# Unread matmuls in the loading phase, earlier loads of two batches, and one place for the second softmax's products

## The chip, the cores and the metric

One core of a Trainium2 chip runs the kernel. The metric is the device time of one execution in microseconds, lower is better. A second, profiled execution gives the trace that the times of single instructions come from.

## The reference

Batch 8, 8 heads, 512 tokens and 32 state rows per head, head size 64; the feed-forward part has 1536 hidden columns. Two softmax attentions are computed between tokens and state, and their results, 544 rows a batch, go through a gated feed-forward layer:

```python
scores = scale * x @ state.T          # 512 x 32 per head
a = softmax(scores); xread = a @ state
scores2 = scale * state @ x.T         # 32 x 512 per head
a2 = softmax(scores2); sread = a2 @ x
y = concat([xread, sread], rows)      # per batch 544 rows of 8 * 64 columns
out = (sigmoid(y @ w_gate) * (y @ w_val)) @ w_out
```

## The kernel before

All tensors are cast to bf16 for TensorE. `xread` is never formed: since `xread @ w = a @ (state @ w)`, the kernel multiplies the small state by the weights once a batch (`sw_wide`, `sw_visit`, result `SW`) and then the transposed probabilities `aT` by `SW` (`gv_mm`, line L283). The sigmoid is a tanh on ScalarE (`gv_th`), the gate product runs on VectorE (`gv_glu`), and `out_mm` (L314) multiplies by `w_out`.

Every instruction's place on its engine is written out by hand (`manual_schedule`): each engine works strictly in the order of the program text, and waits there for what it needs. Tiles come from pools with few buffers; a tile waits for the readers of the buffer that it takes over. In PSUM, `p_gv` has two buffers, `p_sw` four, `p_out` and `p_at` one each. `stg`, which holds x as it is loaded, has three, `Eb` two, `res` four.

**The loading phase** (up to `for b in range(2, B + 1)`) is a list of single calls. Batches 1 and 0 come first: their x is loaded in pieces by SyncE's queue (SP), cast, transposed on TensorE (`xT_mm`, L105), and goes through the scores and the first softmax, while the weights and the state arrive on GpSimd's queue (POOL). `warm(n, place)` (L348) issues n matmuls of 128 x 128 x 128 on a constant tile, into a PSUM tile that nobody reads.

**The steps.** The last loop runs over b = 2 to 8 and, inside, over the twelve column groups f of 128 hidden columns. In step b, group f issues `gv_mm(b, f)`, its tanh and gate product, and one third of an output tile of batch b - 1 (`out_mm(b - 1, f)`). Around this the step prepares the next batch, nb = b + 1:

- groups 0 and 6: `sw_wide(nb, ...)`, state times weights; its copies are spread over the following groups.
- groups 0 to 5 (1 to 6 while b < 4): `row(nb, t)`, the first softmax, ending in `aT_dma(nb)`, four transposing DMAs on SP from `ab` to `aT`.
- groups 7 to 11: `col(nb, t)`, the second softmax, ending in `c_dma(nb)`, two transposing DMAs on SP from `cN` to `Eb`.
- `load_x(b + 3)` on SP in group 8 (b = 2) or 6 (b = 3 and 4); `cast_x(b + 2)` on POOL and `at_xT_dma(b + 2)`, four transposing DMAs on SP, in group 1 (6 for b = 2).
- `sr_mm(b)`, 16 matmuls of 64 columns, the second softmax's product with x, into a PSUM tile `srp`; `sr_cp(b, 0, act)` and `sr_cp(b, 1, vec)` copy it to `XS` on ScalarE and VectorE. For b of 2 and 3 they stand in groups 9 and 10 and use `p_sw`; for b of 4 to 7 in groups 3 and 4, with `p_at`.

Step 7 has no next batch; it runs the second softmax of batches 0 and 1 instead (`col(0, f)`, `col(1, f - 3)`, with `sr_mm(0)` in group 8 and `sr_mm(1)` in group 11). Step 8 does the feed-forward of all `sread` rows, `XS`, in one go (L286).

Of the kernel before, what the change touches and what calls it, by code (L numbers as in the profile page):

```python
# [16 lines left out]
def kernel(  # L17
# [15 lines left out]
    B, H, S, D = x.shape  # L33
# [30 lines left out]
    AT, OU, GV, SWP = (p_at, "at"), (p_out, "outp"), (p_gv, "gv"), (p_sw, "swp")  # L64
# [5 lines left out]
    def load_x(b, eng, parts=1):  # L70
        xf = xfs[b] = stg.tile((128, H, 4, D), FP, name="xf")
        v, n = x[b].rearrange("h (p c) d -> p h c d", c=4), H // parts
        for i in range(parts):
            eng.dma_start(xf[:, n * i:n * i + n], v[:, n * i:n * i + n])

    def load_w(w, lo, n):
        src = (moe_w_gate, moe_w_val)[w].rearrange("(k p) n -> p k n", p=128)
        nc.gpsimd.dma_start((wg, wv)[w][:, :, lo:lo + n], src[:, :, lo:lo + n])
# [9 lines left out]
    def cast_x(b, cp, lo, n):  # L88
        if b not in xbs:
            xbs[b] = xp.tile((128, 4, H, D), BF, name="xb" if b > 1 else "xb01", bufs=3 if b > 1 else 2)  # L90
        cp(xbs[b].rearrange("p c h d -> p h c d")[:, lo:lo + n], xfs[b][:, lo:lo + n])  # L91


    def xT_tile(b):
        if b not in xTs:
            xTs[b] = ap_.tile((128, 4, 4, 128), BF, name="xT" if b > 1 else "xT01")
        return xTs[b]
# [9 lines left out]
    def xT_cp(b, j, cp):  # L107
        cp(xT_tile(b)[:, j], held["xT", b, j])
# [6 lines left out]
    def S_mm(b, i, place, jjs=(0, 1)):  # L115
        if jjs[0] == 0:
            held["S", b, i] = place[0].tile((128, 4, 2, 2, Ns), FP, name="Sp", tag=place[1])
        ps = held["S", b, i]
        for jj in jjs:
            for c in range(4):  # L120
                nc.tensor.matmul(ps[:, c, :, jj], xTs[b][:, 2 * i + jj, c], sTz[:, b, 2 * i + jj], start=True, stop=True)  # L121

    def S_max(b, i):

        if b not in E1s:
            E1s[b] = ap_.tile((128, 4, 2, 4, Ns), FP, name="E1")
        ps = held["S", b, i].rearrange("p c e j n -> p (c e) j n")
        mx = held["mx", b, i] = ap_.tile((128, 8, 2), FP, name="mx")
        nc.vector.tensor_reduce(mx, ps, AX.X, ALU.max)  # L129
# [81 lines left out]
    def sr_mm(b, place):  # L211
        sr = held["sr", b] = place[0].tile((128, 4, 2, Ns), FP, name="srp", tag=place[1])
        Eb = Ebs[b].rearrange("p c e (j n) -> p c e j n", n=Ns)
        for j in range(4):
            for c in range(4):
                nc.tensor.matmul(sr[:, j], xbs[b][:, c, 2 * j:2 * j + 2].rearrange("p h d -> p (h d)"),  # L216
                                 Eb[:, c, :, j], start=(c == 0), stop=(c == 3))
# [32 lines left out]
    def sw_wide(b, v):  # L250

        if b not in SWs:
            SWs[b] = fp.tile((128, 2, 2, dff), BF, name="SW", bufs=2)
        lo = 768 * v
        for k, places in enumerate(((OU, AT), (SWP, SWP), (SWP, SWP))):
            pss = [p[0].tile((128, 512), FP, name="swp", tag=p[1]) for p in places]
            if k < 2:
                sw_mm(pss, b, k, lo, 512, 0)
            else:
                for w in range(2):  # L260
                    sw_mm(pss, b, w, lo + 512, 256, 256 * w)
            for e in range(2):
                if k < 2:
                    sw_left[b, v, k, e] = (SWs[b][:, e, k, lo:lo + 512], pss[e])
                else:
                    sw_left[b, v, k, e] = (SWs[b][:, e, :, lo + 512:lo + 768], pss[e].rearrange("p (w n) -> p w n", w=2))

    def sw_cp(b, lo, w, e, cp):
        cp(*sw_left.pop((b, lo, w, e)))  # L269
# [5 lines left out]
    def gv_mm(b, f, place):  # L275
        n = n_of(b)
        fs = slice(f * 128, (f + 1) * 128)
        pss = []
        for w in range(2):
            ps = place[0].tile((128, 512), FP, name="gvp", tag=place[1])[:, :n]  # L280
            if b < B:
                for g in range(2):
                    nc.tensor.matmul(ps, SWs[b][:, g, w, fs], aTs[b][:, :, g], start=(g == 0), stop=(g == 1))  # L283
            else:
                for j in range(4):
                    nc.tensor.matmul(ps, (wg, wv)[w][:, j, fs], XS[:, j], start=(j == 0), stop=(j == 3))  # L286
            pss.append(ps)
        held["gv", b, f] = pss

    def gv_th(b, f):  # L290

        th = held["th", b, f] = fp.tile((128, 512), FP, name="th")[:, :n_of(b)]
        nc.scalar.activation(th, held["gv", b, f][0], AF.Tanh, scale=0.5)  # L293

    def gv_glu(b, f):
        if b not in glus:
            glus[b] = fp.tile((128, NF, n_of(b)), BF, name="glu", bufs=2, padded_shape=(128, NF, 512))
        nc.vector.scalar_tensor_tensor(glus[b][:, f], held["th", b, f], 1.0, held["gv", b, f][1], ALU.add, ALU.mult)  # L298
# [45 lines left out]
    def warm(n, place):  # L344

        ps = place[0].tile((128, 512), FP, name="warm", tag=place[1])
        for _ in range(n):
            nc.tensor.matmul(ps[:, :128], ones[:, 0], ones[:, 0], start=True, stop=True)  # L348
# [8 lines left out]
    def load_sb(q):  # L357
        sbs[q] = stg.tile((128, 1, 4, D), BF, name="sb", bufs=4)
        nc.gpsimd.dma_start(sbs[q][:, 0], state[2 * q:2 * q + 2].rearrange("b h (u l) d -> (b h u) l d", l=4))
# [5 lines left out]
    def sT_mm(q, place):  # L365
        ps = stp[q] = place[0].tile((128, 4, 64), FP, name="stp", tag=place[1])
        for l in range(4):
            for e in range(2):
                nc.tensor.matmul(ps[e * 64:(e + 1) * 64, l], sbs[q][:, 0, l], ident_e[:, e], start=True, stop=True)
# [74 lines left out]
    load_w(0, 0, 256)  # L444
    cast_x(1, vec, 4, 2)
    nc.vector.memset(sTz, 0.0)
    sT_mm(0, SWP)
    load_x(0, nc.sync, 4)
    cast_x(1, act, 2, 2)
# [10 lines left out]
    cast_x(0, vec, 0, 2)  # L460
    cast_x(0, pool, 4, 2)
    xT_cp(1, 1, act)
    S_mm(1, 0, GV)
    S_max(1, 0)
    xT_cp(1, 3, act)
    S_mm(1, 1, GV)
    S_max(1, 1)
    cast_x(0, act, 2, 2)
# [12 lines left out]
    warm(8, SWP)  # L481
    load_sb(3)
    load_w(0, 512, 512)
    S_mm(0, 0, GV, (0,))
    S_mm(0, 0, AT, (1,))
    S_exp(1, 1)
# [205 lines left out]
    for b in range(2, B + 1):  # L692
        nb = b + 1 if b + 1 < B else None
        for f in range(NF):

            v, q = divmod(f, 6)
            if nb is not None and q == 0:
                sw_wide(nb, v)
                sw_cp(nb, v, 0, 0, act)
                sw_cp(nb, v, 0, 1, act)  # L700
            ahead = nb is not None and q == 0
            for first in (ahead, not ahead):
                if first:
                    gv_mm(b, f, SWP if b == B and f % 2 else GV)
                    gv_th(b, f)
                    gv_glu(b, f)
                elif b < B or f < 9:
                    out_mm(b - 1, f)
            if nb is not None:
                if q == 0:  # L710
                    sw_cp(nb, v, 1, 0, vec)
                if q in (1, 3, 4):
                    k = max(q + 1, 3)
                    sw_cp(nb, v, k // 2, k % 2, act)
                if f == (4 if b > 3 else 10):
                    sr_cp(b, 0, act)
                    sr_cp(b, 1, vec)
                if 0 <= f - (b < 4) < 6:
                    row(nb, f - (b < 4))
                elif f >= 7:  # L720
                    col(nb, f - 7)
                if f == (6 if b > 2 else 8) and nb + 2 < B:
                    load_x(nb + 2, nc.sync, 4 if nb + 3 == B else 1)
                if f == (1 if b > 2 else 6) and nb + 1 < B:
                    cast_x(nb + 1, pool, 0, 4)
                    cast_x(nb + 1, pool, 4, 4)
                    at_xT_dma(nb + 1)
            if b < B and f == (3 if b > 3 else 9):
                sr_mm(b, AT if b > 3 else SWP)
            if b == B - 1:  # L730
                if f == 4:
                    sr_cp(b, 0, act)
                    sr_cp(b, 1, vec)
                for k in range(2):
                    if 0 <= f - 3 * k < 5:
                        col(k, f - 3 * k)
                    elif f == 8 + 3 * k:
                        sr_mm(k, SWP)
                        sr_cp(k, 0, act)
                        sr_cp(k, 1, vec)  # L740
# [33 lines left out]
```

## Time and profile before

| | |
|---|---|
| median of the timed runs | 234.08 us |
| the three timed runs | 233.50, 234.08, 234.56 us |
| profiled execution | 233.25 us |
| its span, first to last instruction | 231.5 us |
| mean granted TensorE clock in it | 0.993 |
| TensorE matmul busy (PE) | 221.3 us, 96% |
| VectorE (DVE) | 138.2 us, 60% |
| ScalarE (ACT) | 143.0 us, 62% |
| GpSimd (POOL) | 71.6 us, 31% |

A row of the timeline has the start from the span's beginning, the length, the engine, the line, the operation, its output and inputs with their shapes, and the number of equal instructions that it merges; in brackets stands how long the engine sat idle ahead of it, and what ended that. SPq and POOLq are issues to DMA queues; their length is the time of issue, not of the transfer. The end of a matmul is modelled: it overlaps the start of the next one, so short waits of PE show as a late start, or as a row that is longer than others of its form, and not as idle time.

### The profile page before, as it was taken

Reading aid. Unit: us, or ns where it says so; the run is one execution under the profiler, and the core shown is the slowest. Engines: PE = TensorE matmul, PEld = TensorE weight load, DVE = VectorE, ACT = ScalarE, POOL = GpSimd, SP = SyncE. Lnnn points to the kernel's source line nnn. Section 1 sums busy time; section 2 is a strip of 40 time slices with the busy share of each in tenths; the row PEclk is TensorE's granted clock in tenths of the full one; section 3 lists DMA queues with packets and bytes.
Section 4 is the critical chain, followed back from the end, with each engine's and each line's share of the span. In section 5 each row is a group of like instructions: output and inputs, shape, how many; then the busy total and the mean of one; then the engine's idle time right before and its main releaser. Section 6 shows DMA issues by size and latency. Waiting matters only on the chain.

```text
span 231.5 us, 4984 instructions
## 1 busy us (share of the span) xinstructions
PE 221.3 (96%) x1887; PEld 110.6 (48%) x1887; DVE 138.2 (60%) x266; ACT 143.0 (62%) x288; POOL 71.6 (31%) x77
## 2 busy tenths in 40 slices
PE   7679999999999999998999999999999999999994
PEld 7463444434544444444444454444444444566743
DVE  0889679766586558754865477648755664422311
ACT  3688787668485857584666767594847655423311
POOL 4986380320515053305330623041302246000001
PEclk9979999999999999999999999999999999999999
DMA  6999969835791459456862844213112312311113
GB/s 204 278 201 287 199 90 202 239 82 125 182 224 50 71 140 224 75 145 187 170 170 55 276 80 128 63 75 91 46 37 93 100 27 76 109 42 70 45 32 107
DMA packets 47271, 29.49 MB, mean 127 GB/s; under 512 B 29872, under 2 KB 42544, under 8 KB 47248
## 3 DMA queue, kind: packets, MB, share of 16 engines
q1 hardware_dynamic: 40096, 21.84, 37.4%
q0 software_dynamic: 6864, 7.14, 16.7%
q8 instruction: 15, 0.25, 0.5%
q10 hardware_dynamic: 288, 0.20, 0.4%
q14 instruction: 8, 0.07, 0.1%
HBM read 18.35 MB, written 8.91 MB: 118 GB/s over the span
## 4 chain that ended last, share of the span: by engine, by line
PE 79%; DVE 7%; DMA 4%; ACT 4%; POOL 2%; issue 2%; SPq 1%; ACTq 0%; DVEq 0%; POOLq 0%
PE outp L314 33%; PE gvp L283 31%; PE gvp L286 5%; PE swp L231 4%; DVE glu L298 3%; DMA Eb<-cN 2%; DMA xf<-in_x_dram 2%; PE srp L216 2%; POOL cN L204 1%; PE cTp L181 1%; ACT th L293 1%; PE outp L334 1%; PE Sp L121 1%; DVE rs L144 1%; ACT SW L269 1%
## 5 line engine op out<-in xcount | busy, mean ns | idle before, releaser
L298 DVE SCALAR_TENSOR_TENSOR glu<-th,gvp 128x512 bf16<-128x512 f32 (+1 forms) x108 | 70.3, 657 | 71.6 <-ACT th L293 52.8
L314 PE MATMUL outp<-wo,glu 128*128 128x512 bf16 x396 | 99.0, 379 | 0.0
L283 PE MATMUL gvp<-aT,SW 128*128 128x512 bf16 x384 | 97.4, 379 | 1.5 <-DMA aT<-ab 0.6
L293 ACT ACTIVATE th<-gvp 128x512 f32<-128x512 f32 (+1 forms) x108 | 61.8, 576 | 52.9 <-PE gvp L283 43.5
L283 PEld LDWEIGHTS <-SW 128*128 128x128 bf16 x384 | 36.3, 98 | 47.0 <-issue 6.2
L314 PEld LDWEIGHTS <-glu 128*128 128x128 bf16 x396 | 36.6, 98 | 40.7 <-issue 2.8
L204 POOL TENSOR_SCALAR cN<-cE,rc 128x512 bf16<-128x512 f32 x16 | 24.9, 1564 | 64.5 <-DVE rc L201 55.7
L269 ACT CAST SW<-swp 128x512 bf16<-128x512 f32 x74 | 41.1, 586 | 3.9 <-PE swp L231 2.8
L318 ACT ACTIVATE res<-outp 128x512 f32<-128x512 f32 x33 | 19.7, 597 | 17.2 <-PE outp L314 17.1
L152 POOL TENSOR_TENSOR ab<-E,ri 128x512 bf16<-128x512 f32 x16 | 16.7, 1047 | 42.5 <-DVE ri L146 34.8
L91 POOL CAST xb<-xf 128x1024 bf16<-128x1024 f32 (+1 forms) x14 | 13.6, 987 | 15.0 <-PE gvp L283 6.6
L269 DVE CAST SW<-swp 128x512 bf16<-128x512 f32 x22 | 14.8, 681 | 0.9 <-PE swp L231 0.9
L196 ACT ACTIVATE cE<-cTp,nb 128x512 f32<-128x512 f32 x16 | 11.1, 694 | 1.2 <-POOL cN L204 1.2
L144 DVE TENSOR_REDUCE rs<-E 128x16 f32<-128x512 f32 x16 | 10.8, 676 | 0.8 <-ACT E L137 0.7
L188 DVE TENSOR_REDUCE cm<-cTp 128x1 f32<-128x512 f32 x16 | 10.9, 683 | 0.4 <-PE cTp L181 0.4
L137 ACT ACTIVATE E<-E 128x512 f32<-128x512 f32 x16 | 10.1, 638 | 1.6 <-DVE E L134 1.6
L129 DVE TENSOR_REDUCE mx<-Sp 128x16 f32<-128x512 f32 x16 | 10.7, 675 | 0.4 <-PE Sp L121 0.4
L134 DVE TENSOR_TENSOR E<-Sp,mx 128x512 f32<-128x512 f32 x16 | 10.9, 685 | 0.1
L325 POOL DMA_DIRECT2D out_dram<-res x2 | 1.1, 550 | 29.7 <-ACT res L318 29.7
L231 PE MATMUL swp<-wg,sTc 64*32 64x512 bf16 (+1 forms) x192 | 8.4, 328 | 0.2
L231 PEld LDWEIGHTS <-sTc 64*32 64x32 bf16 x384 | 4.8, 91 | 7.4 <-issue 4.7
L121 PEld LDWEIGHTS <-xT 128*128 128x128 bf16 x128 | 6.0, 100 | 4.4 <-issue 1.0
(62 smaller groups left out, 134.3 us busy)
## 6 DMA issues: line engine op xcount, KB each, us to landing
out_dram<-res SPq DMA_DIRECT2D x31, 256.0 KB, 2.4
xf<-in_x_dram SPq DMA_DIRECT2D x12, 256.0 KB, 4.5
xf<-in_x_dram SPq DMA_DIRECT2D x3, 1024.0 KB, 6.6
wo<-in_moe_w_out_dram POOLq DMA_DIRECT2D x3, 512.0 KB, 8.5
wv<-in_moe_w_val_dram POOLq DMA_DIRECT2D x2, 512.0 KB, 9.1
wg<-in_moe_w_gate_dram POOLq DMA_DIRECT2D x2, 512.0 KB, 9.7
xf<-in_x_dram POOLq DMA_DIRECT2D x2, 512.0 KB, 8.1
xf<-in_x_dram POOLq DMA_DIRECT2D x1, 1024.0 KB, 12.6
```

The lines of the kernel that those rows point to most:

```text
L91: cp(xbs[b].rearrange("p c h d -> p h c d")[:, lo:lo + n], xfs[b][:, lo:lo + n])
L144: nc.vector.tensor_reduce(rs, halfE(b, i), AX.X, ALU.add)
L152: eng.tensor_tensor(abs_[b].rearrange("p c e (j n) -> p (c e) j n", n=Ns)[:, ce, 2 * i:2 * i + 2], halfE(b, i)[:, ce], ri[:, ce].unsqueeze ...
L204: eng.tensor_scalar(held["cN", b][:, e], held["cE", b, e], rc, None, op0=ALU.mult)
L231: nc.tensor.matmul(pss[e][j * Ns:(j + 1) * Ns, o:o + n], sTc[rows, b, j] if b > 1 else sTz[rows, b, j, e], (wg, wv)[w][rows, j, lo:lo + n] ...
L269: cp(*sw_left.pop((b, lo, w, e)))
L283: nc.tensor.matmul(ps, SWs[b][:, g, w, fs], aTs[b][:, :, g], start=(g == 0), stop=(g == 1))
L286: nc.tensor.matmul(ps, (wg, wv)[w][:, j, fs], XS[:, j], start=(j == 0), stop=(j == 3))
L293: nc.scalar.activation(th, held["gv", b, f][0], AF.Tanh, scale=0.5)
L298: nc.vector.scalar_tensor_tensor(glus[b][:, f], held["th", b, f], 1.0, held["gv", b, f][1], ALU.add, ALU.mult)
L314: nc.tensor.matmul(ops[b, c], glus[b][:, f, c * 128:(c + 1) * 128], wo[:, f], start=(f == 0), stop=(f == NF - 1))
L318: nc.scalar.activation(res, ops[b, c], AF.Copy, scale=0.5)
```

## The change

Four calls of `warm`, with 10, 8, 2 and 4 matmuls on `p_gv`, are added to the loading phase: ahead of `sT_mm(0)`, of `S_mm(1, 0)`, of `S_mm(1, 1)` and of `S_mm(0, 0)`. In the steps, x of batches 5 and 6 is loaded in group 3 of steps 2 and 3, where it was group 8 and group 6. `sr_mm` stands in group 9 of all steps, always on `p_sw`, and its copies in group 10.

```diff
     nc.vector.memset(sTz, 0.0)
+    warm(10, GV)
     sT_mm(0, SWP)
...
     xT_cp(1, 1, act)
+    warm(8, GV)
     S_mm(1, 0, GV)
     S_max(1, 0)
     xT_cp(1, 3, act)
+    warm(2, GV)
     S_mm(1, 1, GV)
...
     load_w(0, 512, 512)
+    warm(4, GV)
     S_mm(0, 0, GV, (0,))
...
-                if f == (4 if b > 3 else 10):
+                if f == 10:
                     sr_cp(b, 0, act)
                     sr_cp(b, 1, vec)
...
-                if f == (6 if b > 2 else 8) and nb + 2 < B:
+                if f == (6 if b > 3 else 3) and nb + 2 < B:
                     load_x(nb + 2, nc.sync, 4 if nb + 3 == B else 1)
...
-            if b < B and f == (3 if b > 3 else 9):
-                sr_mm(b, AT if b > 3 else SWP)
+            if b < B and f == 9:
+                sr_mm(b, SWP)
             if b == B - 1:
-                if f == 4:
+                if f == 10:
                     sr_cp(b, 0, act)
                     sr_cp(b, 1, vec)
```

## The prediction

> **What bounds the kernel now.** I read the page first, then the clock by windows, then PE's timeline step by step, and last the queues behind PE's waits. "Step b" is a turn of the last loop, "group" its column group f.
>
> ```profile
> span 231.5 us, 4984 instructions
> ...
> PE   7679999999999999998999999999999999999994
> ```
> The profiled execution took 233.25 us: this span and 1.75 around it. The median of the three timed runs is 234.08, 0.83 above. PE is busy in nearly every slice (tenths of a slice), so the time is PE's own work and the holes in it, some of which hide inside a "9". The three windows around the thin slices (length, each engine's busy us and count, granted clock, DMA share, GB/s):
>
> ```profile
> 7.06:10.48 3.42, 1.82 (x28) 1.39 (x29) 2.96 (x7) 2.19 (x6) 3.10 (x6) 1.00 1.27 274
> 10.48:13.89 3.41, 3.00 (x52) 2.67 (x56) 3.31 (x8) 2.63 (x5) 2.36 (x5) 0.50 1.44 196
> 13.89:17.30 3.41, 2.17 (x81) 1.49 (x62) 2.53 (x6) 3.25 (x7) 3.41 (x5) 1.00 1.30 203
> ```
> After 3.42 us with PE busy for 1.82, the clock is 0.50 for 3.41 us; after 3.41 us with 2.17 it stays whole. The timeline of all engines there:
>
> ```profile
> 6.05 0.32 PE L369 MATMUL stp<-ident,sb 128*64 128x64 bf16 x8
> ...
> 8.55 0.28 PE L121 MATMUL Sp<-sTz,xT 128*128 128x64 bf16 x4 [0.70 <-DVE xT L108]
> ...
> 11.91 1.06 PE L348 MATMUL warm<-ones 128*128 128x128 bf16 x8
> ...
> 12.76 0.64 PE L121 MATMUL Sp<-sTz,xT 128*128 128x64 bf16 x8
> ...
> 14.03 2.05 ACT L269 CAST SW<-swp 128x512 bf16<-128x512 f32 x4 [0.92 <-PE swp L231]
> ...
> 15.45 0.62 PE L159 MATMUL aTp<-ident,ab 128*128 128x128 bf16 x8 [0.91 <-POOL ab L152]
> ```
> What comes last there is POOL: aTp at 15.45 waited 0.91 for POOL's ab. PE at half clock lies beside that. But ACT's four SW copies end at 16.08, just as aTp does (16.07), so ACT has no slack in front of aT.
>
> In the steps I look for late matmuls. A group of four 512-column products starts 0.86 us after the one before it, and its row lasts 1.04 (130.68 below).
>
> ```profile
> 76.48 0.63 PE L216 MATMUL srp<-Eb,xb 128*128 128x64 bf16 x16
> ...
> 105.96 1.02 PE L283 MATMUL gvp<-aT,SW 128*128 128x512 bf16 x4 [0.61 <-DMA aT<-ab]
> ...
> 112.47 1.03 PE L283 MATMUL gvp<-aT,SW 128*128 128x512 bf16 x4
> 113.92 0.63 PE L216 MATMUL srp<-Eb,xb 128*128 128x64 bf16 x16 [0.43 <-DMA Eb<-cN]
> ...
> 118.71 1.32 PE L283 MATMUL gvp<-aT,SW 128*128 128x512 bf16 x4
> ...
> 130.68 1.04 PE L283 MATMUL gvp<-aT,SW 128*128 128x512 bf16 x4
> ...
> 166.99 1.31 PE L283 MATMUL gvp<-aT,SW 128*128 128x512 bf16 x4
> ...
> 190.71 1.20 PE L283 MATMUL gvp<-aT,SW 128*128 128x512 bf16 x4
> ...
> 192.82 1.31 PE L283 MATMUL gvp<-aT,SW 128*128 128x512 bf16 x4
> ```
> The head of step 4 waits **0.61** for DMA aT. srp (the products of sr_mm) should follow the group of 112.47 at 113.33 and starts at 113.92: **0.59** lost to DMA Eb. Group 6 of steps 4 to 6 is late inside itself: 118.71 is the first and 166.99 the last of three such rows, **0.27 each**. In step 7 the starts 190.71 and 192.82 lie 2.11 apart where two groups take 1.73, and the second row is 0.27 too long: **0.65**.
>
> **The change, part by part.** *sr_mm and sr_cp of steps 4 to 7 go from groups 3 and 4 to groups 9 and 10.* Nothing is added: 16 products of 64 columns move within their step. Eb, wanted at 113.33, is then wanted six groups of 1.73 later, so the 0.59 goes. In group 9 sr_mm takes a p_sw buffer, as in steps 2 and 3: the row of 76.48 has no wait, so I cost the new place at nothing. The place of the copy matters more. DVE's timeline in step 4:
>
> ```profile
> 117.29 0.29 DVE L221 CAST XS<-srp 64x128 bf16<-64x128 f32 x1
> 117.62 0.69 DVE L144 TENSOR_REDUCE rs<-E 128x16 f32<-128x512 f32 x1
> ...
> 118.69 0.69 DVE L298 SCALAR_TENSOR_TENSOR glu<-th,gvp 128x512 bf16<-128x512 f32 x1
> ```
> The glu that ends at 119.38 frees the p_gv buffer that the second half of group 6 waits for. XS, the copy of sr_cp, stands in front of it, 0.33 from start to start. Without it glu ends 0.33 earlier, and the 0.27 goes; 0.06 behind it DVE is late again. I take 0.25 each, 0.75 for three; bounds 0 (ACT's tanh holds glu instead) and 0.81.
>
> In step 7 the same copy stands in the same place, on DVE and then ACT:
>
> ```profile
> 189.25 0.29 DVE L221 CAST XS<-srp 64x128 bf16<-64x128 f32 x1
> ...
> 191.50 0.69 ACT L196 ACTIVATE cE<-cTp,nb 128x512 f32<-128x512 f32 x1 [1.23 <-POOL cN L204]
> ```
> XS delays the reciprocal of col(0, 4), with it POOL's cN, and cE on ACT waits 1.23 for cN's buffer, with the next tanh behind it. Without XS that line is 0.32 earlier relative to PE, since the 16 products leave group 3 for both alike. I take 0.32 of the 0.65; bounds 0.1 and 0.65.
>
> One wait is new. c_dma(1) in group 7 wrote into the Eb buffer that sr_mm(7) had left in group 3. With sr_mm(7) in group 9 the buffer that comes free first is sr_mm(0)'s, in group 8: in the built program SP's transposes for Eb(1) now wait for it.
>
> ```profile
> 195.31 2.73 SPq L209 DMA_TRANSPOSE Eb<-cN  x2
> ...
> 195.70 0.63 PE L216 MATMUL srp<-Eb,xb 128*128 128x64 bf16 x16
> ...
> 201.34 0.63 PE L216 MATMUL srp<-Eb,xb 128*128 128x64 bf16 x16
> ```
> sr_mm(0) ends at 196.33, so SP's issue of 195.31 slides 1.1 us. Behind it on SP stand output stores, whose four res buffers PE is not waiting for. The issue then ends near 199.1. Eb is wanted by sr_mm(1) at 201.34, and later still by the 16 products of sr_mm(7) that now precede it. That leaves over 2.2 from the issue's end to landing, where aT below needs 1.4 (104.49 to 105.9). Cost 0; bound +2.0, with the 4.2 that Eb took behind x6, below.
>
> *The loads: x5 from group 8 of step 2 to group 3, x6 from group 6 of step 3 to group 3.* SP, POOL, one row of PE and one of the chain:
>
> ```profile
> 63.27 5.38 SPq L320 DMA_DIRECT2D out_dram<-res  x2
> 76.81 6.46 SPq L113 DMA_TRANSPOSE xT<-xb  x4
> ...
> 80.88 3.10 POOL L204 TENSOR_SCALAR cN<-cE,rc 128x512 bf16<-128x512 f32 x2 [7.27 <-ACT th L293]
> 84.01 0.39 SPq L74 DMA_DIRECT2D xf<-in_x_dram  x1
> ...
> 84.74 0.40 PE L121 MATMUL Sp<-sTz,xT 128*128 128x64 bf16 x8
> 85.24 3.04 SPq L209 DMA_TRANSPOSE Eb<-cN  x2
> ...
> 90.61 2.02 POOL L91 CAST xb<-xf 128x1024 bf16<-128x1024 f32 x2 [6.63 <-PE gvp L283]
> 92.66 5.57 SPq L113 DMA_TRANSPOSE xT<-xb  x4
> ...
> 94.61 1.05 POOL L152 TENSOR_TENSOR ab<-E,ri 128x512 bf16<-128x512 f32 x1 [0.93 <-DVE ri L146]
> ...
> 99.43 5.06 SPq L173 DMA_TRANSPOSE aT<-ab  x4
> ...
> 104.60 0.52 SPq L74 DMA_DIRECT2D xf<-in_x_dram  x1
> ...
> 108.14 5.65 DMA Eb<-cN
> ```
> x5 is issued at 84.01; POOL's cast of it starts 6.6 later, at 90.61. SP's transposes of x5 wait for that until 92.66, two stores wait behind them, and aT of batch 4 gets its turn at 99.43 although POOL had its ab at 95.66. That is the 0.61. In the changed order x5 stands between the two stores of 63.27, so it is issued about 64 and has landed by 71. Its cast follows cN at 84.0, its transposes follow Eb's issue at 88.3 and end near 93.9. Then come a store, the 1 MB of x6, a store, and aT at 95.7, held by ab alone: 3.7 earlier. The last of it was there at 105.96, so now at 102.2, for a need at 105.35. Against that, x6 now precedes aT: Eb, issued from 108.14 behind x6's 104.60, landed 5.65 after, 4.2 after its issue's end. aT's issue would end at 100.8; with 4.2 it lands at 105.0, which is still in time. x6 itself (94.6 + 6.6) has then landed at 101.2. I take -0.61; bounds -0.61 and +0.4 (6 us in place of 5.65 and another 0.7 from slower transposes). x6's earlier cast takes a wait from POOL in step 4 that nothing of PE's hung on.
>
> *24 unread matmuls.* Eight took 0.85 from 11.91 to 12.76 at half clock, so 0.053 each at full clock. Ten ahead of sT_mm need 0.53: PE waits 0.23 there already, and the other 0.3 falls into the 1.60 us that PE is idle in the next window. Eight and two around S_mm(1, 0) need 0.53, and PE is idle for 0.70 ahead of 8.55. Four ahead of S_mm(0, 0) need 0.21. The window 7.06 to 10.48 then has 2.35 in place of 1.82, above the 2.17 that kept the clock, so I expect no 0.50. The gain of that is 0 all the same, as POOL's ab holds the chain. If the clock does fall, the four cost 0.42, and ACT's SW copies and aT behind them come that much later. Bounds -0.2 (an execution in which the slow stretch takes in the 0.62 of aTp) and +0.5; I take 0.
>
> The Trainium skill (TensorE: Matmul & The Clock Gate, "Why this matters for your kernels") asks only that PE have no idle gap above about 3 us. By that rule the clock would not have dropped here, and the 24 would be bare cost. The trace disagrees: 0.70 is the longest gap ahead of this drop.
>
> **Sum.** 0.59 + 0.75 + 0.32 + 0.61 = 2.27 off 233.25: 231.0 for an execution like the profiled one, **231.8** for the median.
>
> **The rivals.** (a) *The slow clock stays, or moves behind 13.89,* and the four matmuls lie on ACT's line: +0.5, 232.3. For it: at full clock the 3.00 busy us of 10.48 to 13.89 shrink towards half, below 2.17, and the next window may be the slow one. Against it: the added matmuls. The skill's rule above books them as cost too. (b) *The waits only change hands:* tanh holds glu in group 6, and aT is as late behind x6 as it was. 0.59 + 0.32 are left: 233.2, no change that can be told. For it: DVE has 0.06 of slack. (c) *Slower: transposes land late behind the moved loads.* x5 now precedes batch 3's aT and x4's xT on SP. The latter's issue ends at 83.27 and S_mm(4, 0) reads it at 84.74: with 1.4 to landing nothing is left over. If it took 4.2, as Eb did behind x6, PE would wait 2.7 there, and aT of batch 4, which must land by 105.35, would lose the 0.61 gain and 0.4 more: 2.7 + 0.4 - 0.59 - 0.75 - 0.32 = +1.4, 235.5. It turns slower from a wait of 1.3 at 84.74 on. Against it: x5 has 7.7 us from 64 to the start of that aT (76.81 less 5.1) and takes 6.6. (d) *It does not do what it says* is excluded by the built order, in which the 24 matmuls, both loads and the four srp stand where the text puts them.
>
> **How the numbers follow.** Forecast 0.60 (own range 231.0 to 232.5), (a) 0.14, (b) 0.16, (c) 0.10. Within 0.5% (1.17 us, about what a measurement can tell from no change) lies (b). Faster 0.74, same 0.16, slower 0.10. The range begins at 230.7, where every bound is met (0.59 + 0.81 + 0.65 + 0.61 + 0.2 = 2.9) and some of the 0.83 between profile and median goes too, and ends at 233.3, behind (b); it leaves out (c) and about a tenth more.
>
> **What would show it.** Right: no window at 0.50; group 6 of steps 4 to 6 at 1.04; no wait of PE for aT or Eb; the cast of x5 at 84 and aT of batch 4 issued near 95; Eb(1) issued after sr_mm(0), with no wait at sr_mm(1). Wrong: a PE wait for xT in group 1 of step 3, or for Eb at the end of step 7; a slow clock after 13; glu still late in group 6.

## The result, and the profile after

| | before | changed |
|---|---|---|
| median of the timed runs | 234.08 us | 230.75 us |
| all runs | 233.5 to 234.56 us | 230.65 to 232.1 us |
| profiled execution | 233.25 us | 230.65 us |
| its span | 231.5 us | 228.9 us |

The ratio of the runs is 0.987, 95% interval 0.983 to 0.992: faster by 3.3 us, which is clear of the noise, though small (1.3%). It is 1.1 below the forecast, and 0.05 inside the low end of its range. The profiled executions lie 2.60 apart.

The page of the changed kernel (span, and PE's row by slices), then its clock by windows, to be read as the three windows of before:

```profile
span 228.9 us, 5007 instructions
...
PE   8868999999999999999999999999999999999994
```
```profile
8.59:12.01 3.42, 2.47 (x39) 1.92 (x39) 2.98 (x6) 2.93 (x7) 2.94 (x7) 1.00 1.42 197
12.01:15.42 3.41, 1.93 (x60) 1.47 (x57) 3.31 (x9) 3.17 (x7) 2.52 (x3) 1.00 1.40 201
15.42:18.83 3.41, 2.88 (x59) 1.82 (x60) 2.57 (x6) 2.70 (x7) 2.96 (x5) 1.00 1.26 205
```
The clock is whole, and the head is no faster for it. PE's timeline there:

```profile
11.82 0.83 PE L348 MATMUL warm<-ones 128*128 128x128 bf16 x12
...
15.62 0.62 PE L159 MATMUL aTp<-ident,ab 128*128 128x128 bf16 x8 [1.62 <-POOL ab L152]
```
aTp is at 15.62 where it was at 15.45 (the first piece of x was cast 0.17 later); PE at full clock only waits longer for POOL's ab, 1.62 in place of 0.91. From aTp to the last sw_wide of the loading phase (51.29 in before, 51.46 now) it is 35.84 us in both.

PE in step 4 (its head, group 3 and group 6), in group 6 of step 6, and in step 7:

```profile
105.45 1.04 PE L283 MATMUL gvp<-aT,SW 128*128 128x512 bf16 x4
...
111.97 1.03 PE L283 MATMUL gvp<-aT,SW 128*128 128x512 bf16 x4
112.83 1.03 PE L314 MATMUL outp<-wo,glu 128*128 128x512 bf16 x4
...
117.16 1.04 PE L283 MATMUL gvp<-aT,SW 128*128 128x512 bf16 x4
...
164.87 1.04 PE L283 MATMUL gvp<-aT,SW 128*128 128x512 bf16 x4
...
187.80 1.02 PE L314 MATMUL outp<-wo,glu 128*128 128x512 bf16 x4 [0.23 <-ACT res L318]
188.66 1.03 PE L283 MATMUL gvp<-aT,SW 128*128 128x512 bf16 x4
...
192.97 0.63 PE L216 MATMUL srp<-Eb,xb 128*128 128x64 bf16 x16
...
199.09 0.63 PE L216 MATMUL srp<-Eb,xb 128*128 128x64 bf16 x16
```
No row waits for aT or Eb, group 6 is at 1.04, and what is left of step 7's hole is 0.23 at 187.80. What set these rows free, on POOL (the cast of x5) and on SP (the loads of x5 and x6, the transposes of aT(4) and of Eb(1)):

```profile
84.09 2.02 POOL L91 CAST xb<-xf 128x1024 bf16<-128x1024 f32 x2
```
```profile
64.18 0.39 SPq L74 DMA_DIRECT2D xf<-in_x_dram  x1
...
92.34 0.39 SPq L74 DMA_DIRECT2D xf<-in_x_dram  x1
...
95.85 5.04 SPq L173 DMA_TRANSPOSE aT<-ab  x4
...
193.69 2.50 SPq L209 DMA_TRANSPOSE Eb<-cN  x2
```
Cut at the starts of sw_wide, and for step 8 at its first product (L286), the two traces compare as follows (us). A later sentence on half a step means one sw_wide to the next:

| stretch | before | changed | difference |
|---|---|---|---|
| up to step 2 | 56.49 | 56.66 | +0.17 |
| steps 2 and 3 | 48.01 | 48.01 | 0 |
| step 4 | 25.40 | 23.86 | -1.54 |
| step 5 | 24.14 | 23.86 | -0.28 |
| steps 6 and 7 | 48.83 | 48.22 | -0.61 |
| step 8, to the last instruction | 28.61 | 28.26 | -0.35 |

### The profile page after: what moved, and what is told of

Same layout as the page of the kernel before. It is cut to its first block, busy times and chain, and to the rows that moved or that the text cites. A ratio compares the mean times of both kernels' runs of the same rounds, so it can differ in the third digit from the quotient of the medians.

```text
span 228.9 us, 5007 instructions
## 1 busy us (share of the span) xinstructions
PE 219.1 (96%) x1885; PEld 111.5 (49%) x1911; DVE 138.0 (60%) x266; ACT 143.1 (63%) x288; POOL 71.4 (31%) x77
## 4 chain that ended last, share of the span: by engine, by line
PE 84%; DMA 7%; ACT 2%; issue 2%; POOL 2%; SPq 1%; DVE 0%; ACTq 0%
PE outp L314 36%; PE gvp L283 34%; PE swp L231 5%; PE gvp L286 5%; DMA wg<-in_moe_w_gate_dram 4%; DMA xf<-in_x_dram 2%; PE srp L216 2%; PE Sp L121 1%; SPq L74 1%; PE outp L334 1%; PE cTp L181 1%; POOL cN L204 1%; ACT res L318 1%; POOL xb L91 1%; ACT SW L269 1%
## 5 line engine op out<-in xcount | busy, mean ns | idle before, releaser
L314 PE MATMUL outp<-wo,glu 128*128 128x512 bf16 x370 | 95.5, 379 | 1.7 <-issue 0.3
L348 PE MATMUL warm<-ones 128*128 128x128 bf16 x87 | 7.6, 256 | 1.0 <-DVE ones L429 1.0
```

What stands on the lines that cost most here:

```text
L314: nc.tensor.matmul(ops[b, c], glus[b][:, f, c * 128:(c + 1) * 128], wo[:, f], start=(f == 0), stop=(f == NF - 1))
```

## The experiments

The kernel before was timed beside each group of kernels: 234.91 (17 runs), 234.35 (23) and 234.08 us (11), always with a wide spread (232.9 to 235.9, and one execution at 237.2). So a time says little below 0.5 us here, and each verdict leans on rows too.

### The changed kernel again, and each part of it

**e0**: the changed kernel.

> The changed kernel once more, beside the others of this group. Theory: 2.4 us of PE's holes gone (1.5 in step 4, 0.3 in each of steps 5 to 7), the loading phase neither faster nor slower: 2.4 to 3.3 below the kernel before, as one of before's executions lost another us to an output store. Rival: part of the 3.3 comes from the loading phase, and then the variants without the 24 matmuls lie above this one.

230.73 us, ratio 0.984 (0.980 to 0.987): some 3.8 us below before, of which the interval allows 3.0 to 4.6, where 2.4 to 3.3 was expected. **e4** leaves the 24 matmuls out of it:

```diff
-    warm(10, GV)
...
-    warm(8, GV)
...
-    warm(2, GV)
...
-    warm(4, GV)
```


> The changed kernel without its 24 unread matmuls; loads and second-softmax products stay as changed. Theory (the 24 are worth nothing, POOL's ab holds the chain at the head): within 0.3 us of the changed kernel, with a stretch of 3.4 us at 0.50 back near 10.5 us. Rival 1 (they earn time by the whole clock): 0.4 to 1.0 slower than the changed kernel. Rival 2 (they are bare cost): 0.3 to 0.5 faster than it.

231.28 us, ratio 0.986 (0.982 to 0.989): 0.55 above e0. That is outside the theory's 0.3 and in rival 1's band of 0.4 to 1.0, but the two intervals overlap, so this pair alone decides nothing. **e3** puts the same four lines into the kernel before.

> The kernel before with the 24 unread matmuls alone. Theory: no stretch at 0.50, the first products with aT still behind POOL's ab near 15.6 us, time within 0.3 us of the kernel before; the waits of step 4 (0.6 for aT, 0.6 for Eb) stay. Rival 1: 0.4 to 1.0 faster than before. Rival 2: 0.3 to 0.5 slower.

233.46 us over 12 runs, ratio 0.995 (0.992 to 0.997): faster, so the theory that the 24 earn nothing falls. But not by what rival 1 says. The windows of e3:

```profile
13.74:17.15 3.41, 1.72 (x56) 1.26 (x55) 2.50 (x6) 2.70 (x6) 3.41 (x5) 1.00 1.30 203
17.15:20.56 3.41, 3.16 (x13) 1.45 (x13) 3.31 (x8) 2.25 (x5) 2.17 (x3) 0.50 1.26 238
```
The slow stretch (a period of 3.41 us at a clock of 0.50) is there all the same. It begins at 17.15, behind the window in which PE waits for ab, and not at 10.48 as in before. e4, without the 24, has it at 17.10. Where it lies decides its price. Two distances show that, one ahead of aTp (from DVE's first cast of x to aTp) and one behind it (from aTp to the last sw_wide of the loading phase):

| slow stretch from | traces | cast to aTp | aTp to sw_wide |
|---|---|---|---|
| none | changed, e0, e2, e5, e7 | 9.59 to 9.71 | 35.84 |
| 10.48, 11.73, 12.06 | before, e11, e1 | 9.58 to 9.72 | 35.84 |
| 10.77 | e9 | 9.59 | 35.96 |
| 16.00 | e6 | 9.73 | 36.10 |
| 17.10 | e4 | 9.58 | 36.33 |
| 17.15 | e3 | 10.20 | 36.49 |
| 17.25 | e8 | 10.06 | 36.51 |
| 17.27 | e10 | 9.62 | 36.51 |

So the stretch costs 0.12 or less where it lies ahead of aTp, and up to 0.67 where PE is itself on the chain.

What the 24 do earn shows at the other end. The last output stores on SP's queue, of e4 and of the changed kernel (two issues in each row):

```profile
223.99 2.23 SPq L325 DMA_DIRECT2D out_dram<-res  x2
```
```profile
224.00 0.78 SPq L325 DMA_DIRECT2D out_dram<-res  x2
```
The DMA queues while those stores run (packets, MB, share of 16 engines), again e4 (221.4 to 228.5 us), then the changed kernel (221.4 to 228.9):

```profile
q1 hardware_dynamic: 576, 0.59, 30.6%
q0 software_dynamic: 64, 0.13, 7.4%
q8 instruction: 1, 0.02, 1.2%
```
```profile
q1 hardware_dynamic: 576, 0.59, 29.6%
q0 software_dynamic: 64, 0.13, 6.1%
```
One 16 KB load of instructions (q8) falls among the last stores of e4, and the issue beside it takes 1.88 us in place of 0.42. In the changed kernel that load comes at 220.2, ahead of them. The same split runs through all traces: the five kernels with the 24 (changed, e0, e3, e5, e8) have no such load there and a last stretch of 28.26 to 28.28 us; the nine traces without them have it, and 28.29 to 28.80, 28.56 on average. So the 24 move the load, and in these traces the shorter end is worth 0.30 on average. That they move it past the stores is luck of the place: the prediction has nothing of it, and no run tries another number of matmuls.

The granted clock of single executions gives a little more. The five traces without a slow stretch are at 1.0, those with one at 0.993 or less. It was 0.998 or above in 13 of 34 executions with the 24 and in 9 of 95 without (e6 left out, as its long wait slows the clock by itself). Within one kernel those executions are shorter on average, by 0.75 us (changed), 0.62 (e0), 0.07 (e3), 0.25 (e5) and 0.44 (e8); weighted by the 13, by 0.39. An estimate from these numbers: a slow stretch fewer in 0.29 of the executions at 0.39 us is 0.11. With the 0.30 that is 0.41 of the 0.55 between e4 and e0. Of the 1.27 (0.54%) between e3 and before, 0.9 stay open; e3's own trace, its slowest execution (234.05), doesn't show them. So that the 24 earn something is measured, and most of the reason is not known.

**e1**: the second softmax's products alone.

```diff
-                if f == (4 if b > 3 else 10):
+                if f == 10:
...
-            if b < B and f == (3 if b > 3 else 9):
-                sr_mm(b, AT if b > 3 else SWP)
+            if b < B and f == 9:
+                sr_mm(b, SWP)
...
-                if f == 4:
+                if f == 10:
```


> The kernel before with sr_mm and sr_cp in groups 9 and 10 of all steps, nothing else. Theory: 0.59 (Eb) + 3 x 0.27 (the copy ahead of glu) + 0.33 (step 7) = 1.7 us faster than before; the wait of 0.6 for aT at the head of step 4 stays, group 6 of steps 4 to 6 has rows of 1.04. Rival 1 (waits change hands, glu is held by tanh): 0.9 faster. Rival 2 (the sr products want a p_sw buffer at a bad moment): under 0.6 faster, with a new wait in group 9.

232.10 us, ratio 0.990 (0.986 to 0.994). PE in step 4:

```profile
106.53 1.02 PE L283 MATMUL gvp<-aT,SW 128*128 128x512 bf16 x4 [0.78 <-ACT SW L269]
...
118.22 1.04 PE L283 MATMUL gvp<-aT,SW 128*128 128x512 bf16 x4
```
Group 6 is right and the wait for Eb gone; the head of step 4 still waits. The row names ACT's SW, but the last of aT landed at 106.40, and in the changed kernel the same row starts while that SW copy still runs. Step 5 lasts as in the changed kernel, and so do steps 6 and 7 together (48.22): the 0.28 in steps 5 and 6 and the 0.33 in step 7 are this part's own. From step 4 to step 7 it saves 1.6 us by the rows, where the theory had 1.7.

### The two loads, one by one

**e2** has both loads in group 3, **e7** x5 alone, **e6** x6 alone, each in the kernel before, which gets one of the three new lines:

```diff
-                if f == (6 if b > 2 else 8) and nb + 2 < B:
+                if f == (6 if b > 3 else 3) and nb + 2 < B:      # e2
+                if f == ({2: 3, 3: 6}.get(b, 6)) and nb + 2 < B: # e7
+                if f == ({2: 8, 3: 3}.get(b, 6)) and nb + 2 < B: # e6
```


> The kernel before with x of batches 5 and 6 loaded in group 3, nothing else. Theory: the wait for aT at the head of step 4 goes (0.6), and the wait for Eb in group 3 of step 4 goes too (0.6), since Eb's transposes no longer stand behind x6; group 6 of steps 4 to 6 keeps its 0.27, step 7 its 0.65: 1.2 us off the profiled 233.25, so some 232.0, and the spread of before's executions goes. Rival 1: aT is as late behind x6 as it was, 0.6 or less gained. Rival 2: the moved loads make the transposes of xT(4) late, a wait in group 1 of step 3 and a time above before's.

232.33 us, ratio 0.992 (0.989 to 0.995). Steps 2 and 3 last 48.02 us, against 48.01 before, so the early x5 makes nothing late there, and rival 2 falls.

> The kernel before with x5 alone in group 3 of step 2; x6 stays in group 6 of step 3. Theory: aT(4) is issued near 94, ahead of x6, and its wait goes (0.6 off); x6 is then issued near 100 and Eb's transposes after it at 105 to 107, so the wait for Eb shrinks or stays: 0.6 to 1.2 us off the 233.25. Rival: the wait for aT had another cause than the late x5, and stays.

232.49 us, ratio 0.992 (0.990 to 0.995). In both, the first half of step 4 lasts 12.17 in place of 13.44, a gain of 1.26 by the rows. e7's SP, then its PE:

```profile
95.33 5.04 SPq L173 DMA_TRANSPOSE aT<-ab  x4
100.48 0.52 SPq L74 DMA_DIRECT2D xf<-in_x_dram  x1
...
105.75 3.56 SPq L209 DMA_TRANSPOSE Eb<-cN  x2
```
```profile
104.93 1.04 PE L283 MATMUL gvp<-aT,SW 128*128 128x512 bf16 x4
...
112.31 0.63 PE L216 MATMUL srp<-Eb,xb 128*128 128x64 bf16 x16
...
117.10 1.31 PE L283 MATMUL gvp<-aT,SW 128*128 128x512 bf16 x4
```
x5 alone takes both waits away, for aT and for Eb, as x6 is then issued at 100.48 and lands at 106.69, while Eb's transposes are still being issued; Eb landed at 110.56, for a need at 112.31. Moving x6 as well adds nothing. Group 6 stays late at 1.31, as that is the other part's. And x6 moved without x5:

> The kernel before with x6 alone in group 3 of step 3; x5 stays in group 8 of step 2. Theory: x6 now stands ahead of aT(4), which is late already, so aT waits for x6's megabyte as Eb did (4.2 us behind its issue's end where 1.4 is usual): the wait at the head of step 4 grows by 2 to 3 us, Eb's wait goes (-0.6): 1.5 to 2.5 us slower than before. Rival: transposes behind a load are not late for the load's sake, the wait at the head stays at 0.6, and the kernel is 0.6 faster than before.

237.32 us, ratio 1.012 (1.008 to 1.016): 3.0 slower in the median, 0.5 more than the theory's upper end; the traced execution (239.54) is one of its slowest. SP, PE and the windows of e6:

```profile
99.48 0.39 SPq L74 DMA_DIRECT2D xf<-in_x_dram  x1
99.97 0.67 SPq L320 DMA_DIRECT2D out_dram<-res  x1
100.74 6.04 SPq L173 DMA_TRANSPOSE aT<-ab  x4
```
```profile
111.45 1.86 PE L283 MATMUL gvp<-aT,SW 128*128 128x512 bf16 x4 [5.84 <-DMA aT<-ab]
113.11 1.91 PE L314 MATMUL outp<-wo,glu 128*128 128x512 bf16 x4
```
```profile
104.75:108.16 3.41, 0.86 (x33) 0.37 (x32) 0.76 (x2) 1.43 (x3) 3.10 (x2) 1.00 1.73 133
108.16:111.57 3.41, 0.12 (x1) 0.14 (x2) 0.00 (x0) 0.00 (x0) 2.02 (x2) 0.50 1.11 165
111.57:114.99 3.42, 3.42 (x12) 1.20 (x11) 1.29 (x2) 0.60 (x1) 0.00 (x0) 0.50 1.54 155
```
The rival falls. aT, issued 1.3 us behind x6's megabyte, landed at 111.31, 4.5 after its issue's end. PE waited 5.84 for it. The clock fell inside that wait, at 108.16, so that the first two groups behind it took 1.86 and 1.91 in place of 1.03. The same order, load ahead of aT, is free in the changed kernel: there aT is issued 3.5 us after x6, landed at 101.99, 1.1 after its issue's end, and is wanted 9.6 us after its issue begins. Whether the larger distance from x6 or the lighter traffic makes it land sooner, no run separates.

### The copy in front of glu

**e5**: the changed kernel with DVE's share of the old place put back alone.

```diff
+    spare = wp.tile((128, 4, Ns), BF, name="spare")
...
+                if f == 4 and b > 3:
+                    vec(spare[64:128], XS[64:128, :, 64:96])
```


> The changed kernel with one unread DVE copy of 64 partitions x 128 (XS into a spare tile) put into group 4 of steps 4 to 6, where sr_cp's copy stood: DVE's cost alone, without the products or ACT's half. Theory (the copy ahead of glu made group 6 late): the second half of group 6 of steps 4 to 6 lasts 1.31 again in place of 1.04, a half of each of these steps 11.96 in place of 11.71, 0.75 us slower than the changed kernel. Rival (the 16 products leaving group 3, or ACT's half of the copy, made the difference): no change.

231.50 us, 0.77 above e0, which ran in another group. DVE, then PE, in step 4:

```profile
115.55 0.43 DVE L721 COPY spare<-XS 64x128 bf16<-64x128 bf16 x1
...
116.95 0.63 DVE L299 SCALAR_TENSOR_TENSOR glu<-th,gvp 128x512 bf16<-128x512 f32 x1
```
```profile
116.96 1.26 PE L284 MATMUL gvp<-aT,SW 128*128 128x512 bf16 x4
```
The second half of step 4 lasts 12.37 in place of 12.15, that of step 5 12.38, and steps 6 and 7 together 0.22 more: 0.67 in all, for a copy and nothing else. So DVE's copy alone brings back 0.22 of the 0.28 a step, and the rival (PE's products or ACT's half) is not needed for more than the rest. The copy is not quite the old one: it takes 0.43 us, where that took 0.29.

### The rest of step 7

**e8**: the changed kernel with a third buffer for cE, ACT's output that POOL's cN reads.

```diff
-        ex = held["cE", b, e] = ap_.tile((128, 512), FP, name="cE")
+        ex = held["cE", b, e] = ap_.tile((128, 512), FP, name="cE", bufs=3)
```


> The changed kernel with three buffers for cE in place of two: in step 7 ACT's cE waited for the buffer that POOL's cN still read. Theory: ACT's waits for cN in step 7 (0.37 and 0.43 in the changed kernel) go, and with them PE's hole of 0.2 at 187.8: 0.2 to 0.4 us faster than the changed kernel. Rival: the next thing that holds ACT there (the transposed products of col) is as late: no change within 0.1.

230.46 us, ratio 0.985 (0.982 to 0.988). PE's row, where 0.23 was lost at 187.80:

```profile
187.46 1.03 PE L283 MATMUL gvp<-aT,SW 128*128 128x512 bf16 x4
188.33 1.03 PE L314 MATMUL outp<-wo,glu 128*128 128x512 bf16 x4
```
The hole is gone, ACT's cE waits no more (it waited 0.37 and 0.43 in the changed kernel), and steps 6 and 7 last 48.01 in place of 48.22: a gain of 0.2 by the rows; in the times it is too small to tell from the changed kernel.

### The kernel before, traced again

**e9, e10, e11** are the kernel before, unchanged.

> The kernel before itself, as one more variant: what the comparison tells of no change, and a second trace of it. Its median among the others was 234.9, 1.6 above the execution profiled first (233.25), and its executions spread over 4 us where those of the changed kernel spread over 1.5. Theory: the extra is in the two waits for transposes of step 4 (0.6 for aT and 0.6 for Eb in the first trace, longer here) and in where the slow clock falls at the head. Rival: it is spread evenly over the steps. Ratio to before 1.00 within 0.4%.

> One more trace of the kernel before. The two so far are of executions of 233.25 and 233.54, while half of its executions take over 234.5. Theory 1: a typical execution waits longer for DMA at the head of step 4 and in its group 3 (aT, Eb), 1 to 2 us more than 1.2 together. Theory 2: the slow clock lies behind 14 us at the head, where PE is on the chain, and costs 0.5 to 1 us there (0.65 in the trace with the 24 matmuls alone). Which row has grown tells.

> The same once more, since a single trace may again be of a short execution. Theory 1: the waits for aT and Eb in step 4 have grown. Theory 2: the start of step 1 is late, with the slow clock behind 14 us.

Measured beside itself (e9, 12 runs, 235.22 us), the ratio is 1.003 (1.000 to 1.006). The traced executions took 233.54, 234.33 and 233.65. Of e11 and e10, PE at the head of step 4 and at srp:

```profile
105.95 1.02 PE L283 MATMUL gvp<-aT,SW 128*128 128x512 bf16 x4 [0.50 <-DMA aT<-ab]
...
114.56 0.63 PE L216 MATMUL srp<-Eb,xb 128*128 128x64 bf16 x16 [1.08 <-DMA Eb<-cN]
```
```profile
106.91 1.02 PE L283 MATMUL gvp<-aT,SW 128*128 128x512 bf16 x4 [0.74 <-ACT SW L269]
...
115.06 0.63 PE L216 MATMUL srp<-Eb,xb 128*128 128x64 bf16 x16 [0.61 <-DMA Eb<-cN]
```
In e10 the row names ACT's SW again, and the last of aT landed at 106.77. The first half of step 4 lasts 13.44, 13.23, 13.75 and 13.97 in the four traces of before (the first, e9, e10, e11), and 11.71 in each of the five with both parts (changed, e0, e4, e5, e8). Both theories hold a part: waits that grow by up to 0.5, and in e10 a slow stretch from 17.27 at 0.67. Executions of 235 to 237 us were not caught in a trace, and what they add stays open.

## Why the prediction was right, point by point

- **sr_mm's wait for Eb, 0.59, and x5's 0.61 for aT: right, and doubly covered.** Step 4 lost 1.54; 0.28 of it is group 6, 1.26 the two waits (1.20 forecast). The worst case that the text allowed, aT landing 4.2 after its issue's end, did not come: it was 1.1. x6 went out at 92.34 and not at 94.6, so aT was issued 3.5 us behind it and not 1.1. e7 shows what the text did not say: x5 alone removes Eb's wait too, and e1 that the new place does so alone. The credits overlap; their sum in the changed kernel does not.
- **The copy ahead of glu, 3 x 0.25: right.** 0.28 in step 5 and in step 6, and e5 gives the mechanism. tanh did not take over, so rival (b) is out.
- **Step 7, 0.32 of 0.65: right.** 0.61 less step 6's 0.28 is 0.33; the cE buffer that the text named holds the next 0.2 (e8).
- **The new wait of Eb(1): right.** It is issued at 193.69, behind sr_mm(0) of 192.97, and the row of 199.09 has no wait.
- **The 24 matmuls, 0: the step that was wrong.** The text took the windows of the one trace as fixed, but their place differs from execution to execution. So "no 0.50" held for the traced execution by luck, and not as a rule (e3, e8). That the head gains nothing from a whole clock was right for a slow stretch ahead of aTp and wrong for one at 17. The 24 earn more than the bound of -0.2 (1.27 in e3), and something like the bound of +0.5 was met too. The first ten stand behind fifteen that were there; the 25 in e3, and in e0:

```profile
5.07 2.44 PE L348 MATMUL warm<-ones 128*128 128x128 bf16 x25
```
```profile
4.90 1.56 PE L348 MATMUL warm<-ones 128*128 128x128 bf16 x25
```
That is 0.098 us each in e3 and 0.062 in e0, where 0.053 was counted: at the start they go at about half the rate, until the point at which the trace's record of the clock begins (6.91 us in e3, 7.01 in e8, 4.14 in e0). In e3 and e8 the state's first transposes come at 7.44 and 7.48, and aTp 10.20 and 10.06 after DVE's first cast of x, where all other traces have 9.58 to 9.73: 0.4 to 0.5 lost. That the slow matmuls cause this delay is argued from the order of the rows; no run varies them alone. And the gain at the end, 0.35 in the pair of traces, was not thought of.
- **Rival (a)** was a place, not a case: the stretch at 17.2 costs 0.65 to 0.67 (forecast 0.5), with the 24 or without. **Rival (c)** did not come: xT(4) has no wait in the changed kernel. But its mechanism is real, and e6 shows its price when the order is wrong.
- **The page of the skill** (the Trainium skill, TensorE: Matmul & The Clock Gate, "Why this matters for your kernels"), with its gap of about 3 us, names a gap that no trace here shows at the head, where the clock fell all the same (0.70 us is the longest gap ahead of the fall in before, 0.45 in e1 and e11). e6 has a gap above it, 5.84 us, and the clock fell in it, when PE had been idle for 2.6.
- **The sum.** 2.27 were forecast off the profiled execution, and it lost 2.60: 1.54 + 0.28 + 0.61 = 2.43 in the steps, 0.35 at the end, less 0.17 at the head. The median lost 0.73 more, since the 0.83 by which before's median stood above its profile did not carry over: it is 0.10 now. 0.73 + 0.33 is the whole difference between forecast and result. Part of the 0.73 may be the waits for DMA, which vary by 0.7 between the four traces of before and which the change removed whole; the longer executions were not traced. So the steps were forecast well, while the median lies at the low end of the range through two gains that the sum had not counted.

## What to carry to other kernels

A transfer that engines wait for should be asked for when nothing large was queued just ahead; one load that is late (x5) made two waits, and a load pulled ahead of a late transpose (x6 alone) made one of 5.84 us. When a wait for DMA is removed, the median may gain more than a single trace shows, since the wait differs from execution to execution (by 0.7 us in step 4 here). In this kernel, whose PE is full, a copy of 0.3 us on another engine cost 0.28, what it delayed of the instruction that frees PE's buffer. A forecast for the clock at the head of a program should not rest on the place of the windows in one trace.

## What the runs showed of the hardware

- The clock changes by periods of 3.41 us, whose place differs from one execution to the next: in every trace the changes lie whole multiples of 3.41 apart (before: 3.65, 10.48, 13.89). A period at the head with PE busy for 1.65 (e8), 1.70 (e6), 1.72 (e3, e9), 1.80 (e10), 1.82 (before) or 1.87 us (e4) was followed by one at 0.50; one with 1.91 (e7), 1.93 (changed), 1.97 (e2), 2.03 (e5), 2.10 (e0) or 2.17 (before) was not. But 2.10 (e11) and 2.15 (e1) were followed by a slow one too, so PE's busy time alone doesn't settle it, and what else counts stays open. The longest idle gap in the periods that brought the slow clock at the head was 0.45 to 1.71 us. The periods of e1 and of e0 (columns as before), the first followed by 0.50, the second not:

```profile
8.64:12.06 3.42, 2.15 (x33) 1.61 (x33) 2.91 (x6) 2.93 (x7) 2.94 (x7) 1.00 1.38 189
```
```profile
14.38:17.79 3.41, 2.10 (x51) 1.28 (x52) 2.53 (x6) 2.70 (x6) 3.41 (x5) 1.00 1.27 204
```
- Instructions are loaded while the program runs, in transfers of 16 KB (queue q8). With such a load among the last stores, one issue on SP took 1.08 us (e11) to 1.88 us (e4) where 0.42 or less is usual. Twenty-four matmuls more at the start of the program moved that load from 224.5 (e4) to 220.2. That the load is of PE's own instructions is argued from this shift, not shown.
